# A shared PSUM copy and a closed-up product order in a Winograd-style matrix product

## The chip, the cores and the metric

The kernel runs on one core of one Trainium2 chip. The metric is the device time of one execution in microseconds, the median of several runs. One execution is also recorded by the hardware profiler; its instruction times are what the profile shows.

## The reference

Input `x` is 8 × 3584 tokens of 192 channels. A causal depthwise convolution with 7 taps (8 heads, softmax of the taps) comes first. Each token is then sent to one of 8 experts, and the expert is a two-layer network with 1024 hidden units. Cut to what matters:

```python
# convolution: out[s] = sum over k of softmax(weight)[head, k] * x[s + k - 6]
logits = x @ w_gate                          # (B, S, 8)
local_gate = sigmoid(x @ w_local)
for b in range(B):
    for s in range(S):
        fresh_e = argmax(logits[b, s])
        e = fresh_e if s == 0 or local_gate[b, s] < 0.5 else prev_e
        prev_e = e
        p = softmax(logits[b, s])
        h = maximum(x[b, s] @ w1[e], 0.0)     # 192 -> 1024
        out[b, s] = p[e] * (h @ w2[e])        # 1024 -> 192
```

## The kernel before, in words

All is float32. The 28672 tokens are taken in 16 groups of 1792. For each group the kernel convolves on VectorE (`conv`, line 423, with one small step per head on ScalarE, line 413), computes the gate and the place of every token on VectorE (`route`), and scatters the tokens' rows by GpSimd into a table in device memory sorted by expert (`put`, line 828). TensorE multiplies blocks of 128, 256 or 512 tokens of one expert. Blocks 0 to 27 have 128 tokens, 28 to 70 have 256, **71 to 93 have 512** (the large blocks), and smaller ones follow. Convolution and routing of later groups ("side work") run on VectorE beside the products of blocks that are already complete.

The order on each engine is the order in which the code issues its instructions (a manual schedule); nothing is moved by a planner. How much side work stands at a place of a block is set by budgets: `step(t)` takes steps of routing or convolution until their nominal costs reach `t` us, and an overdraft is taken off the next call. In a large block there are four such calls, with the budgets `SIDE = (2.4, 4.5, 2.0, 1.8)`: the first inside the hidden layer's product (not in block 71), the second behind it, the third and fourth in the output product, behind each half's first eviction. Side work is done when the last group's tables are made.

A large block goes as follows.

- `turn_late` (line 1135) transposes the block's rows on VectorE; `combine_x` (lines 1186 to 1191) makes the sums of token pieces there, `combine_w` (lines 1168 to 1172, 1177) the sums of weight pieces on GpSimd.
- `seven` (lines 1194 to 1247) makes the hidden layer. Of the three 64-channel pieces of the input two are multiplied by seven products in place of eight, in Winograd's way, and the third is added. `times` (line 1208, matmuls at line 1211) issues eight matmuls: two column pieces `j`, two row halves; each row half has a PSUM bank of its own. Three PSUM tiles of two banks are used: `xb`, `yb` (both named `ps` in the profile) and `wbk` (named `xps`). `xb` holds running sums: ScalarE copies it after the first product (line 1217) into `h11` and after the second (line 1225) into `h12`; then the third product is accumulated on it. `h22` is copied from `yb` (line 1223).
- Between the second product and the third, `wbk` takes eight matmuls of `a12, b21` and four of `a13, b31`; the other four of these follow the third product. Then VectorE adds (`h22` at line 1231, `h11` at 1233, `h12` at 1243) and ScalarE applies the ReLU (lines 1235, 1244 to 1246). The weight and token pieces `t2`, `s2` and so on, the hidden pieces, all lie in tiles that the profile names `xg`, `hot`, `hT`.
- `output_late` (matmuls at line 1261) makes the output layer in two halves of 256 tokens; ScalarE (line 1271) and VectorE (line 1276) scale the results, and GpSimd scatters them to the output (line 1096). `ensure` loads the rows of the blocks ahead on SP (lines 986, 991), once their tokens are scattered.

Of the kernel before, what the change touches and what calls it, by code (L numbers as in the profile page):

```python
# [111 lines left out]
def kernel(  # L112
# [10 lines left out]
    nc = tc.nc  # L123
# [264 lines left out]
    def halves():  # L388
        return [(half, slice(half * DR, (half + 1) * DR)) for half in range(2)]
# [431 lines left out]
    def put(behind=None):  # L821


        if not to_put:
            return
        g, rows, to = to_put.pop(0)
        nc.gpsimd.nop()
        ins = nc.gpsimd.indirect_dma_start(  # L828
            out=slots[:, :], in_=rows, in_offset=None,
            out_offset=bass.IndirectOffsetOnAxis(ap=to, axis=0)).ins  # L830
        if behind is not None:
            tc.add_manual_dep(ins, behind.ins.name, SYNC, reason="scatters apart")
        if puts:
            tc.declare_no_dep(ins, group="puts", reason="slots of their own")
        if g:
            tc.declare_no_dep(ins, group="gets", reason="those slots were full before")
        puts.append((g, ins))
        tc.add_to_no_dep_group("puts", ins)
        tc.add_to_no_dep_group(f"puts{g}", ins)
# [299 lines left out]
    def pieces(n):  # L1139


        return [room[f"h{k}"][:, :4 * n * P].rearrange("p (h j s) -> p h j s", h=2, j=2)
                for k in range(4)]
# [50 lines left out]
    def seven(wb, wt, weight_then, xT, xc, rows_then, weights_next):  # L1194


        one, two = slice(0, HU * P), slice(HU * P, KQ * P)
        h11, h12, h21, h22 = pieces(HU)
        b11, t1, b21, b22, b31, b32 = [wb[:, WB + k * 2 * P:WB + (k + 1) * 2 * P]
                                       for k in range(6)]  # L1200
        t2, t3, t4 = wt
        a11, s1, a12, a22, a13, a23 = [xT[:, d, s] for d in range(KD) for s in (one, two)]
        s3, s2, s4, s5 = xc
        xb, wbk, yb = [pool.tile([P, 2, 512], F32, name=name).rearrange(
            "p h (j s) -> p h j s", j=2)
            for pool, name in ((late_p[0], "ps"), (xps_p, "xps"), (late_p[1], "ps"))]

        def times(to, a, b, first=False, js=range(2)):
            for j in js:
                for half, rows in halves():  # L1210
                    ins = nc.tensor.matmul(to[:, half, j, :], lhsT=b[rows, j * P:(j + 1) * P],  # L1211
                                           rhs=a[rows, :], start=(first and j == 0), stop=True,
                                           skip_group_check=True)
            return ins

        weight_then(times(xb, a11, b11, True))
        nc.scalar.copy(h11, xb)
        ins = times(yb, s1, t1, True)
        if held:
            held.pop(0)(ins)  # L1220
        rows_then()
        times(yb, a23, b32)
        nc.scalar.copy(h22, yb)
        times(xb, s2, t2)
        nc.scalar.copy(h12, xb)
        put(times(wbk, a12, b21, True))
        times(wbk, a13, b31, js=[0])
        if st["block"] > FIRST:
            step(SIDE[0], early=1)
        put(times(xb, s3, t3))  # L1230
        nc.vector.tensor_tensor(h22, xb, h22, op=Alu.add)
        times(wbk, a13, b31, js=[1])
        nc.vector.tensor_tensor(h11, wbk, h11, op=Alu.add)  # L1233
        for side in range(2):
            nc.scalar.activation(h11[:, side], h11[:, side], Act.Relu)  # L1235
        times(yb, s4, b22)
        put(times(yb, s5, b32))
        times(xb, a22, t4)
        wt = weights_next()
        next(wt)  # L1240
        put(times(xb, a23, b31))
        next(wt)
        nc.vector.tensor_tensor(h12, yb, h12, op=Alu.add)
        nc.scalar.activation(h12, h12, Act.Relu)
        nc.scalar.activation(h21, xb, Act.Relu)
        nc.scalar.activation(h22, h22, Act.Relu)
        return [[h11, h12], [h21, h22]], wt

    def output_late(n, wb, xg, hT, rows_next=None, between=None):

        for part, h in enumerate(hT):
# [21 lines left out]
            if n == KQ:  # L1273
                step(SIDE[2 + part], late_p[0] if part == 0 else None)
            for k in range(m):
# [10 lines left out]
    late_p = []  # L1286
    LEAD = 2
    LATE = 3
    SIDE = (2.4, 4.5, 2.0, 1.8)
    st = {"block": 0, "conv": 1, "cgen": None, "route": 1, "rgen": None, "routed": 1,  # L1290
          "due": False, "hot": False, "since": 0, "bank": None, "over": 0}

    def start_conv():
        g = st["conv"] + 1

        free = not any(p[0] <= g - 3 for p in to_put)
        if (st["cgen"] is None and g < NPART and g <= st["route"] + LEAD and free
                and (g != 3 or g in x_in and st["block"] > LATE + 2)):
            st["conv"] = g
            st["cgen"] = conv(g, x_in.pop(g))  # L1300
            next(st["cgen"])

    def conv_op():
        c = next(st["cgen"], None) if st["cgen"] else None
        if c is None:
            st["cgen"] = None
        return c

    def start_route():
        done = st["conv"] - (st["cgen"] is not None)  # L1310
        if st["rgen"] is None and st["route"] < done:
            st["route"] += 1
            st["rgen"] = route(st["route"])

    def route_op():
        c = next(st["rgen"], None)
        if c is None:
            st["rgen"] = None
            st["routed"] = PADS if st["route"] == LAST else st["route"]
        return c  # L1320

    def step(time, bank=None, early=0, force=False):

        start_route()
        start_conv()
        go = st["rgen"] is not None
        if st["due"]:
            go = (not late_p and st["block"] < FIRST - 1
                  or bank is not None and (force or st["since"] < st["block"]))
            if go:  # L1330
                st["due"], st["bank"] = False, bank
        time += st["over"]
        while time > 0:
            c = route_op() if go else conv_op()
            if c is None:
                if not go:
                    break
                go = False
            elif c == "pe":
                st["due"], st["since"], go = True, st["block"] - early, False  # L1340
            elif c == "hop":
                go = False
            elif c == "placed":
                pass
            else:
                time -= c + 0.05 if go and late_p else c
        st["over"] = min(time, 1.5) if late_p else 0
# [87 lines left out]
    for i, (_, n, _, _) in enumerate(blocks):  # L1435
# [12 lines left out]
        def weights_next():  # L1448
            return combine_w(wbs[i + 1]) if n_next == KQ else iter([None] * 5)
# [25 lines left out]
        if n == KQ:  # L1475
            hT, wt = seven(wbs[i], wt, weight_then, xT, xc, lambda: ensure(i), weights_next)
        else:
            hT = hidden_late(n, wbs[i], xT)
        if n_next:
            xT = turn_late(n_next, xgs[i + 1][0])  # L1480
        if n == KQ:
            step(SIDE[1])
        wts, xcs = [], []
# [116 lines left out]
```

## Time and profile before

| | |
|---|---|
| median of 3 runs | 1312.17 us (1308.29 to 1316.62) |
| profiled execution, its own time | 1309.78 us |
| its span, first to last instruction | 1308.1 us |
| granted TensorE clock | 0.998 |
| large blocks | 695.8 to about 1177 us |
| TensorE matmuls at line 1211 in `seven` | 2024, 88 in each of 23 blocks |
| copy of the second sum, line 1225 | 23 times, 1.02 us each |

The profile gives one execution. A row of the timeline holds the start in us, the length in us, the engine, the line, the operation, the tile written and those read, and how many instructions are merged into it; in brackets the idle time of the engine ahead of it and what ended it. PE is TensorE's matmuls, PEld its weight loads, DVE VectorE, ACT ScalarE, POOL GpSimd, SP the queue that issues loads. A row of groups holds the count, the busy time, the mean length in ns, and the idle time ahead of the group with what ended most of it. A row of waits names who waited for whom, the total in us, the number of times, and sometimes the longest. A row on one line gives the shortest, median and longest instruction in ns.

### The profile page before, as it was taken

To read this page: it belongs to the slowest core of one execution; us is meant where nothing else is said; L and a number is where in the kernel's file an instruction comes from. 1 tells how busy PE (TensorE), PEld (TensorE's weight loads), DVE (VectorE), ACT (ScalarE), POOL (GpSimd) and SP (SyncE) were. 2 spreads that over 40 slices of the span, in tenths; PEclk is the share of its full clock that TensorE was granted. 3 is DMA by queue.
4 is the path that set the end of the run, shared out by engine and by line. 5 is a ranking of instruction groups with operands and counts; after the bars stand their busy time and mean duration, and the time that the engine had idled before them with its cause. 6 is when DMAs were issued, how large, how long until landed. Compare 5 with 4: busy or idle time off the path is not lost. (4 is left out here: it accounts for less than half of the span.)

```text
span 1308.1 us, 39979 instructions
## 1 busy us (share of the span) xinstructions
PE 1276.2 (98%) x15750; PEld 1206.7 (92%) x15750; DVE 956.1 (73%) x2602; ACT 617.5 (47%) x1407; POOL 553.1 (42%) x619
## 2 busy tenths in 40 slices
PE   9899999999999999999999999999999999999997
PEld 7798999999999999899999899999999899999996
DVE  5888898889888788788988998898857844431111
ACT  5345555445555645456463454454434434342332
POOL 4444443534344444444435633654462664421211
PEclk9999999999999999999999999999999999999999
DMA  5789988857767767667696655555455637536894
GB/s 197 272 342 387 373 345 347 296 201 270 259 213 263 257 219 259 215 231 259 206 282 174 181 163 154 149 150 151 125 171 113 194 108 189 155 95 193 268 326 156
DMA packets 130243, 291.18 MB, mean 223 GB/s; under 512 B 87936, under 2 KB 104759, under 8 KB 114306
## 3 DMA queue, kind: packets, MB, share of 16 engines
q1 hardware_dynamic: 107728, 243.35, 56.6%
q0 software_dynamic: 22320, 45.22, 10.2%
q8 instruction: 126, 2.06, 0.7%
q14 instruction: 67, 0.55, 0.1%
q10 hardware_dynamic: 2, 0.00, 0.0%
HBM read 242.92 MB, written 46.07 MB: 221 GB/s over the span
## 5 line engine op out<-in xcount | busy, mean ns | idle before, releaser
L423 DVE SCALAR_TENSOR_TENSOR y_sb<-x_sb,c,y_sb 128x336 f32<-128x336 f32 x672 | 384.5, 581 | 33.3 <-ACT y_sb L413 11.0
L1068 PE MATMUL yps<-wb,hT 64*128 64x192 f32 x3648 | 318.6, 326 | 5.2 <-ACT hT L1056 3.0
L1047 PE MATMUL hps<-xT,wb 64*128 64x256 f32 (+1 forms) x3408 | 315.4, 336 | 2.6 <-issue 1.3
L828 POOL DMA_INDIRECT slots<-y_sb,posi x228 | 227.9, 1000 | 208.9 <-PE yps L1068 150.3
L1261 PE MATMUL ps<-wb,hot 64*128 64x192 f32 x3680 | 309.7, 324 | 2.1 <-issue 1.8
L1261 PEld LDWEIGHTS ps<-wb,hot 64*128 64x128 f32 x3680 | 299.3, 187 | 9.4 <-ACT hot L1235 5.0
L1068 PEld LDWEIGHTS yps<-wb,hT 64*128 64x128 f32 x3648 | 297.4, 187 | 10.2 <-ACT hT L1056 5.1
L1047 PEld LDWEIGHTS hps<-xT,wb 64*128 64x128 f32 x3408 | 283.2, 187 | 23.6 <-issue 3.6
L1096 POOL DMA_INDIRECT out_dram<-o_sb,head x115 | 120.6, 1049 | 296.7 <-DVE o_sb L1276 270.9
L1056 ACT ACTIVATE hT<-hps 128x512 f32<-128x512 f32 (+1 forms) x284 | 130.4, 510 | 161.0 <-PE hps L1047 116.5
L1096 POOL DMA_INDIRECT out_dram<-o_sb,xg x114 | 117.1, 1028 | 207.8 <-DVE o_sb L1082 112.4
L1271 ACT ACTIVATE o_sb<-ps,head 128x192 f32<-128x192 f32 x115 | 43.0, 418 | 205.2 <-PE ps L1261 178.9
L1276 DVE SCALAR_TENSOR_TENSOR o_sb<-ps,head,o_sb 128x192 f32<-128x192 f32 x115 | 43.2, 411 | 111.2 <-ACT o_sb L1271 108.6
L1029 ACT COPY xT<-xps 64x256 f32<-64x256 f32 (+4 forms) x284 | 105.1, 370 | 9.5 <-PE yps L1068 2.2
L1078 ACT ACTIVATE o_sb<-yps,xg 128x192 f32<-128x192 f32 x114 | 43.3, 418 | 125.2 <-PE yps L1068 96.9
L1135 DVE STREAM_TRANSPOSE xT<-y_sb 128x768 f32<-128x768 f32 (+1 forms) x65 | 54.8, 870 | 61.7 <-PE ps L1156 31.2
L1211 PE MATMUL ps<-xT,wb 64*128 64x256 f32 x736 | 88.5, 377 | 1.0 <-DVE xT L1187 1.0
L1211 PEld LDWEIGHTS ps<-xT,wb 64*128 64x128 f32 x736 | 75.3, 187 | 4.9 <-issue 2.2
L1082 DVE SCALAR_TENSOR_TENSOR o_sb<-yps,xg,o_sb 128x192 f32<-128x192 f32 x114 | 43.4, 412 | 33.1 <-ACT o_sb L1078 27.5
L1235 ACT ACTIVATE hot<-hot 128x512 f32<-128x512 f32 x46 | 26.4, 622 | 83.6 <-DVE hot L1233 61.1
L1156 PE MATMUL ps<-xT,wb 64*128 64x128 f32 (+1 forms) x912 | 64.5, 294 | 0.5 <-DVE xT L1135 0.5
L1156 PEld LDWEIGHTS ps<-xT,wb 64*128 64x128 f32 x912 | 62.6, 188 | 1.2 <-DVE xT L1135 1.1
(281 smaller groups left out, 1337.8 us busy)
## 6 DMA issues: line engine op xcount, KB each, us to landing
wb<-in_w_dram SPq DMA_DIRECT2D x109, 1536.0 KB
x_sb<-in_x_dram SPq DMA_DIRECT2D x14, 1920.0 KB
y_sb<-slots SPq DMA_DIRECT2D x92, 192.0 KB
xg<-slots SPq DMA_DIRECT2D x43, 195.0 KB
wb<-in_w_dram SPq DMA_DIRECT2D x12, 512.0 KB
slots<-y_sb,posi POOLq DMA_INDIRECT x228
x_sb<-in_xb_dram SPq DMA_DIRECT2D x4, 768.0 KB
y_sb<-slots SPq DMA_DIRECT2D x60, 48.0 KB
```

The source lines that it names most:

```text
L423: nc.vector.scalar_tensor_tensor(cols(h), chans(h, k), c[:, h, k:k + 1], cols(h), Alu.mult, Alu.add)
L828: ins = nc.gpsimd.indirect_dma_start(out=slots[:, :], in_=rows, in_offset=None, out_offset=bass.IndirectOffsetOnAxis(ap=to, axis=0)).ins
L1029: copied = nc.scalar.copy(a, b)
L1047: ins = nc.tensor.matmul(hps[half][:, j, w], lhsT=wb[rows, f0:f0 + P], rhs=xT[rows, d, w], start=(d == 0 and j == 0), stop=(d == KD - 1), ...
L1056: nc.scalar.activation(hT[:, m:m + 2, w], hps[half][:, :, w], Act.Relu)
L1068: ins = nc.tensor.matmul(yps[half][:, k * D:(k + 1) * D], lhsT=hT[rows, m, k * P:(k + 1) * P], rhs=wb[rows, WA + m * D:WA + (m + 1) * D], ...
L1082: nc.vector.scalar_tensor_tensor(o_sb[:, k, :], y[k][1], xg[:, k, 0:1], o_sb[:, k, :], Alu.mult, Alu.add)
L1096: sent = nc.gpsimd.indirect_dma_start(out=out, in_=o, in_offset=None, out_offset=bass.IndirectOffsetOnAxis(ap=xg.bitcast(I32)[:, k, 1:2], ...
L1135: nc.vector.transpose(xT.rearrange("p d (j t) -> p j d t", t=Q)[:, js], rows[:, js].rearrange("p j (d t) -> p j d t", t=Q))
L1156: nc.tensor.matmul(hps[:, half, j, :], lhsT=wb[rows, f0:f0 + P], rhs=xT[rows, d, :], start=(d == 0 and j == 0), stop=(d == KD - 1), skip_g ...
L1211: ins = nc.tensor.matmul(to[:, half, j, :], lhsT=b[rows, j * P:(j + 1) * P], rhs=a[rows, :], start=(first and j == 0), stop=True, skip_gro ...
L1261: ins = nc.tensor.matmul(yps[:, half, k * D:(k + 1) * D], lhsT=h[two][rows, side, j, k * P:(k + 1) * P], rhs=wb[rows, f * D:(f + 1) * D], ...
```

## The change

In `seven`, the copy of the second sum is cut in two: ScalarE copies the first bank of `xb` into the first half of `h12`, VectorE the second bank into the second half. VectorE's half is issued behind the first stretch of side work of the block. That stretch is issued earlier in the code, ahead of the products into `wbk`, and its budget goes from 2.4 to 1.8. The third product is issued behind the eight matmuls of `a12, b21`; all eight matmuls of `a13, b31` follow it.

```diff
-        def times(to, a, b, first=False, js=range(2)):
-            for j in js:
+        def times(to, a, b, first=False):
+            for j in range(2):
                 for half, rows in halves():
...
         times(xb, s2, t2)
-        nc.scalar.copy(h12, xb)
-        put(times(wbk, a12, b21, True))
-        times(wbk, a13, b31, js=[0])
+        nc.scalar.copy(h12[:, 0], xb[:, 0])
         if st["block"] > FIRST:
             step(SIDE[0], early=1)
+        nc.vector.tensor_copy(h12[:, 1], xb[:, 1])
+        put(times(wbk, a12, b21, True))
         put(times(xb, s3, t3))
         nc.vector.tensor_tensor(h22, xb, h22, op=Alu.add)
-        times(wbk, a13, b31, js=[1])
+        times(wbk, a13, b31)
         nc.vector.tensor_tensor(h11, wbk, h11, op=Alu.add)
...
-    SIDE = (2.4, 4.5, 2.0, 1.8)
+    SIDE = (1.8, 4.5, 2.0, 1.8)
```

## The prediction

> **What bounds the kernel now.** I read the page first: who is busy, and where in the span.
>
> ```profile
> PE 1276.2 (98%) x15750; PEld 1206.7 (92%) x15750; DVE 956.1 (73%) x2602; ACT 617.5 (47%) x1407; POOL 553.1 (42%) x619
> ...
> PE   9899999999999999999999999999999999999997
> ...
> DVE  5888898889888788788988998898857844431111
> ```
>
> TensorE is the bound from end to end, so an edit is worth what it adds to or takes from TensorE's waits. VectorE is busy eight tenths until slice 33, so whatever is given to it there stands in a queue. The change sits in the 23 large blocks (I number them 71 to 93, as in the list of blocks), which fill 695.8 to 1177. Next I read the timeline of one that has no side work, block 88:
>
> ```profile
> 1059.45 1.49 PE L1211 MATMUL xps<-xT,wb 64*128 64x256 f32 x12
> ...
> 1059.78 1.02 ACT L1225 COPY hot<-ps 128x1024 f32<-128x1024 f32 x1
> ...
> 1060.85 1.13 PE L1211 MATMUL ps<-xg 64*128 64x256 f32 x8
> ...
> 1061.82 0.60 PE L1211 MATMUL xps<-xT,wb 64*128 64x256 f32 x4
> ...
> 1062.10 1.23 DVE L1231 TENSOR_TENSOR hot<-ps,hot 128x1024 f32<-128x1024 f32 x1 [4.37 <-PE ps L1211]
> ...
> 1062.25 1.89 PE L1211 MATMUL ps<-hT,wb 64*128 64x256 f32 x16
> ...
> 1063.98 1.03 PE L1211 MATMUL ps<-xT,xg 64*128 64x256 f32 x8
> ...
> 1064.84 1.03 PE L1211 MATMUL ps<-xT,wb 64*128 64x256 f32 x8
> ...
> 1065.71 0.49 PEld L1261 LDWEIGHTS ps<-wb,hot 64*128 64x128 f32 x6 [0.24 <-ACT hot L1235]
> 1065.74 0.60 PE L1261 MATMUL ps<-wb,hot 64*128 64x192 f32 x4
> ```
>
> Call A the start of the twelve filler matmuls (1059.45). Sixteen matmuls take 1.73 us (1062.25 to 1063.98), so one costs 0.108 and twelve 1.30. The third product starts at A+1.40 as soon as the 1.02 us copy L1225 lets go of the second sum. So the copy costs 0.10 us in this block; the filler hides the rest. L1231 follows at A+2.65, the output product at A+6.29.
>
> ```profile
> PEld ps L1211 <- ACT hot L1225: 8.2, 23, 1.5
> ```
>
> The chain of waits makes it look bigger: 8.2 us in 23 waits, 0.36 each. That is weight-load idle; of block 88's share 0.10 is lost pace. 23 blocks at 0.10 are **2.3 us, about all there is to win** in undisturbed blocks.
>
> **The copy, halved.** Durations for 128x512 out of PSUM:
>
> ```profile
> L1056 ACT ACTIVATE hT<-hps 128x512 f32<-128x512 f32 x172 | 93.0, 594 | 111.0 <-PE hps L1047 94.9 <-remote 9.0 <-PE xps L394 7.1
> ```
> ```profile
> L269 ACT COPY z<-hps x9: 532/533/550, 12.5 to 27.5; 128x448 f32<-128x448 f32 x9
> L269 DVE COPY z<-hps x3: 624/625/625, 12.1 to 15.3; 128x448 f32<-128x448 f32 x3
> ```
>
> ScalarE's half: 0.59. VectorE's half is not in the trace: at least the 0.625 of 448 columns, at most 0.71 in proportion; I take 0.69. ScalarE's half would be done at 1059.78+0.59, and with the 0.05 us from copy end to matmul today (1060.80 to 1060.85) the third product starts at A+0.97 at best, since the shorter filler (eight matmuls, 0.86) is out earlier. Then come 8 matmuls (0.97, with the gap that follows a wait), 8+16+8+8 (4.31): output at A+6.25, against A+6.29. **Gain per undisturbed block: 0.04 us.** The smaller filler takes back nearly all that the faster copy gives. The four matmuls moved behind the third product cost nothing: L1233 needs them only after L1231, 1.2 us later. The step of side work itself now stands ahead of the first filler's scatter and of its matmuls. It issues VectorE's steps, ScalarE's small ones (L413, L642), which follow the copy on ScalarE's queue as before, and now and then a load on SP; it puts nothing on GpSimd's queue, and nothing on TensorE's, because this call gives it no PSUM bank. So its move passes no queue in which another order results; only VectorE's queue changes, by the copy.
>
> **The wait that is added.** VectorE's half stands in VectorE's queue behind the first stretch of side work (convolution and routing of later tokens, nominal 2.4 us now, 1.8 after). Behind that copy stands L1231, which needs the third product; so TensorE now waits for side work that it could ignore before. How late VectorE is, is told by its idle time ahead of L1231:
>
> ```profile
> L1231 DVE TENSOR_TENSOR hot<-ps,hot x23: 1211/1225/1225, 701.8 to 1163.2; 128x1024 f32<-128x1024 f32 x23
> ...
> PE ps L1211: 48.6, 21
> ```
> ```profile
> 701.84 1.23 DVE L1231 TENSOR_TENSOR hot<-ps,hot 128x1024 f32<-128x1024 f32 x1 [1.30 <-PE ps L1211]
> ```
> ```profile
> 788.61 1.23 DVE L1231 TENSOR_TENSOR hot<-ps,hot 128x1024 f32<-128x1024 f32 x1 [2.11 <-PE ps L1211]
> ```
> ```profile
> 956.36 1.23 DVE L1231 TENSOR_TENSOR hot<-ps,hot 128x1024 f32<-128x1024 f32 x1 [3.71 <-PE ps L1211]
> ```
> ```profile
> 978.58 1.22 DVE L1231 TENSOR_TENSOR hot<-ps,hot 128x1024 f32<-128x1024 f32 x1 [2.20 <-PE ps L1211]
> ```
> ```profile
> 1163.19 1.23 DVE L1231 TENSOR_TENSOR hot<-ps,hot 128x1024 f32<-128x1024 f32 x1 [4.37 <-PE ps L1211]
> ```
>
> With an idle time g, VectorE is free at A+2.65−g today. After: 0.6 earlier, plus 0.69 for the copy and 0.05, so the third product starts at A+2.79−g. It breaks even at A+1.01 (A+6.29 less 5.28). **So g has to be 1.78 us; each microsecond short of it is lost on TensorE.** Of the 48.6 us, 6×4.37 belong to blocks 88 to 93, 3.71 to block 83 and 1.30 to block 71 (none with side work ahead of L1231); 17.4 remain for 13 blocks, 1.34 on average. Two blocks, 72 and 73, have no idle time at all.
>
> The sum on TensorE:
> - 13 blocks: 13 × (1.78−1.34) = +5.7. Blocks 75 and 84 (2.11, 2.20) cannot bank their surplus: +0.7. In some blocks the output product already waits today for the chain that L1231 opens, and the change gives that chain room (0.97+0.86 us of products behind the third, against 0.97+0.43):
>
> ```profile
> PEld ps L1261 <- ACT hot L1235: 5.0, 16, 0.6
> ```
>
>  5.0 less 16 × 0.24 (block 88's, part of the pace): −1.2.
> - Block 72:
>
> ```profile
> 720.54 3.37 DVE L423 SCALAR_TENSOR_TENSOR y_sb<-x_sb,c,y_sb 128x336 f32<-128x336 f32 x4
> ...
> 721.82 1.14 PE L1211 MATMUL ps<-xg 64*128 64x256 f32 x8 [0.36 <-ACT hot L1225]
> ...
> 723.83 1.22 DVE L1231 TENSOR_TENSOR hot<-ps,hot 128x1024 f32<-128x1024 f32 x1
> ```
> ```profile
> 727.45 1.86 PE L1261 MATMUL ps<-wb,hot 64*128 64x192 f32 x19 [0.27 <-issue]
> ```
>
>  Four convolution steps fill VectorE until 723.83. One step fewer (0.57) and the copy (0.69) put the third product at about 724.0, the output at 729.3: +1.8. Block 73 looks the same (L1231 at 745.60 without idle time), but a later TensorE lets VectorE catch up: between 0.6 and 1.8, taken as +1.2.
> - Block 71 has no side work to shorten:
>
> ```profile
> 700.12 0.42 DVE L1191 TENSOR_TENSOR hT<-xT 128x256 f32<-128x256 f32 x1
> ```
> ```profile
> 705.48 0.76 PE L1261 MATMUL ps<-wb,hot 64*128 64x192 f32 x6
> ```
>
>  Free at 700.54, copied at 701.23, output at 706.56: +1.1.
> - Seven blocks without side work: 7 × −0.04 = −0.3.
> - The shorter stretch. 0.6 us less in each of some 16 blocks is 9.6 us of side work moved back, against a budget of 10.1 a block: it ends about a block later. Counting the side work's steps off against the budgets (each step carries its nominal cost in the code), block 83's first stretch, empty today, gets three transposes of 0.95:
>
> ```profile
> L606 DVE STREAM_TRANSPOSE z<-y_sb 128x768 f32<-128x768 f32 x42 | 38.3, 953 | 0.4
> ```
>
>  Between 0 and 1.2 for that; taken as +0.6. The last group's scatters slip too; block 90 is the first to need them:
>
> ```profile
> 1087.72 1.84 DVE L1135 STREAM_TRANSPOSE xT<-y_sb 128x768 f32<-128x768 f32 x2 [1.91 <-DMA y_sb<-slots]
> ```
> ```profile
> 1092.89 0.41 DVE L1186 TENSOR_TENSOR xg<-xT 128x256 f32<-128x256 f32 x1
> ```
>
>  The transposes end 3.3 us ahead of the first use: one more scatter, and the load behind it, fit there. Nothing.
>
> Together 5.7+0.7−1.2+1.8+1.2+1.1−0.3+0.6 = **+9.6 us**. The profiled execution took 1309.78 (span 1308.1): 1319.4, said as **1319**. The median shown is 1312.17, 2.4 above it, within the 1308.29 to 1316.62 of its runs; by it the same sum gives 1321.8.
>
> Two prices stay open. Does GpSimd slow the copy? The side work's steps stretch beside it:
>
> ```profile
> L423 DVE SCALAR_TENSOR_TENSOR y_sb<-x_sb,c,y_sb x112: 528/571/1541, 713.9 to 942.4; 128x336 f32<-128x336 f32 x112
> ```
>
> 0.57 grows to 1.54 in the worst case, but L1231, which reads PSUM, keeps 1.211 to 1.225 in all 23. I take no stretch; one of 0.97 in each of some 13 blocks would be +12.6 on top, 1332, the upper end. [...] The lower end: were the copy always in time, 23 × −0.04, −1.2 and 72 and 73 at up to −1.0 each (the pace gap at their output) come to −4.
>
> **Rivals.** (1) **VectorE is in time.** If side work's real steps land early, TensorE never waits for VectorE's half and all blocks look like 88: −4 to +2, about 1308. For it: g averages 2.1 over all 23, ScalarE loses 0.42 us a block, and the changed stretch holds other steps than today's. Against: only 9 of 23 blocks have g of 1.78 or more. [...]
>
> ```profile
> 715.95:737.90 21.95, 20.97 (x219) 19.18 (x218) 20.38 (x32) 9.48 (x14) 13.21 (x14) 1.00 0.54 154
> ...
> 908.30:928.50 20.20, 20.20 (x220) 19.20 (x218) 17.97 (x60) 8.45 (x12) 7.95 (x9) 1.00 0.51 139
> ...
> 1056.00:1076.20 20.20, 20.20 (x219) 19.20 (x218) 8.76 (x14) 8.45 (x12) 12.71 (x14) 1.00 0.37 128
> ```
>
> (stretch, its length, then busy time of PE, PEld, DVE, ACT, POOL.) [...] (2) **VectorE becomes the bound.** Between its copy and L1231 it must now idle about 1.3 us (third product and hand-over, 1062.10−1060.85), and side work cannot use that. Where busy time plus 1.3 plus today's other waits exceeds the block, lateness is carried over, as between 72 and 73. From a block of 20.2 it decides at about 18.5 busy, close to the 17.97 above. All 15 side-work blocks behind 72 at block 73's 1.2 make 18, with 72 (1.8) and 71 (1.1): +21, about 1331. (3) The change doesn't do what it says, because the wait for ScalarE's half remains: that is in the 0.97 above, and gives no time of its own.
>
> **The numbers.** Forecast (+3 to +13): 0.58. Rival 1: 0.24. Rival 2: 0.18. Range 1306 (rival 1) to 1332 (rival 2, and the stretched copy). One per cent, 13 us, is about what a measurement of this kernel tells from no change. None of the cases reaches 13 us faster: 0.02. Slower by more: rival 2 and the forecast's upper edge counted from the median, 0.27. Within: 0.71.
>
> **What the profile after would show.** If right: L1231's idle time near 1.2 us in every side-work block, TensorE's wait ahead of the third product put down to VectorE's copy, 0.69 us long, of some 0.5 us in most of blocks 71 to 82 and gone from 89 on, where a block is 20.18 long. ScalarE's half 0.59. Side work in block 88. Wrong if the copy starts right after the second sum in most blocks (rival 1), or if VectorE runs without idle time from block to block (rival 2); or if block 90 waits for its rows.

## The result and the profile after

The changed kernel took 1329.63 us (median of 4 runs, 1329.38 to 1331.55) against 1312.58 for the kernel before on the same chip: ratio **1.0134, 95% interval 1.0100 to 1.0167**. The profiled execution took 1331.55 us, with a span of 1329.6.

The page of the kernel after, busy time and the slices:

```profile
PE 1278.4 (96%) x15750; PEld 1205.2 (91%) x15750; DVE 972.9 (73%) x2625; ACT 607.5 (46%) x1407; POOL 551.4 (41%) x619
...
PE   9899999999999999999998999899999999999996
...
DVE  5888898888888888788887988898857774431111
```

TensorE has about the same work, 1278 us against 1276, in a longer span, so most of the time was lost in waits. Where it was lost is told by the first product of block 71 and of block 93 in the timelines. Before:

```profile
695.81 1.47 PE L1211 MATMUL ps<-xT,wb 64*128 64x256 f32 x12
...
1157.08 2.14 PE L1211 MATMUL ps<-xT,wb 64*128 64x256 f32 x18
```

After:

```profile
694.53 2.75 PE L1211 MATMUL ps<-xT,wb 64*128 64x256 f32 x24
...
1175.11 1.25 PE L1211 MATMUL ps<-xT,wb 64*128 64x256 f32 x10
```

From the one to the other it is 461.27 us before and 480.58 after: **+19.3 of the +21.5 us of span lie in the large blocks** of these two executions (the medians differ by 17). The rest is 1.3 less ahead of the large blocks and 3.5 more behind, of which 2.2 is one wait for a load in a small block. The kernel before doesn't have this wait, nor does a second profile of the kernel after (e9 below):

```profile
PE ps L1156 <- DMA y_sb<-slots: 2.2, 1, 2.2
```

An undisturbed block, one without side work around the copy, shows the new state. Block 93 in the timeline after, with A again the start of the filler:

```profile
1178.56 1.03 PE L1211 MATMUL xps<-xT,wb 64*128 64x256 f32 x8
...
1178.88 0.59 ACT L1225 COPY hot<-ps 128x512 f32<-128x512 f32 x1
...
1179.50 0.69 DVE L1228 COPY hot<-ps 128x512 f32<-128x512 f32 x1 [2.67 <-ACT hot L1225]
...
1180.25 1.13 PE L1211 MATMUL ps<-xg 64*128 64x256 f32 x8 [0.65 <-DVE hot L1228]
1181.21 1.03 PE L1211 MATMUL xps<-xT,wb 64*128 64x256 f32 x8
1181.43 1.23 DVE L1231 TENSOR_TENSOR hot<-ps,hot 128x1024 f32<-128x1024 f32 x1 [1.24 <-PE ps L1211]
```

Read the brackets. VectorE is idle for 2.67 us and has nothing else to do, yet its half of the copy starts 0.03 us after *ScalarE's half ends* (1178.88+0.59=1179.47), not when the second sum is ready. **The halves run one after the other.** Two short copies in a row (0.59+0.69) take longer than the one of 1.02 that they replace, and the filler ahead of the third product is shorter by four matmuls. So the third product starts at A+1.69 (1180.25−1178.56) in place of A+1.40, and TensorE waits 0.65 us. The undisturbed block, 20.22 us long before and 20.18 in the forecast, is 20.82 long.

The waits after, and the three VectorE and ScalarE groups on this path:

```profile
PEld ps L1211 <- DVE hot L1228: 30.9, 23, 2.9
...
DVE hot L1231 <- PE ps L1211: 27.5, 21, 2.2
...
DVE hot L1228 <- ACT hot L1225: 21.7, 12, 2.7
PE ps L1211 <- DVE hot L1228: 21.7, 23, 2.5
```
```profile
L1225 ACT COPY hot<-ps x23: 585/592/592, 698.2 to 1178.9; 128x512 f32<-128x512 f32 x23
L1228 DVE COPY hot<-ps x23: 647/691/692, 699.2 to 1179.5; 128x512 f32<-128x512 f32 x23
...
L1231 DVE TENSOR_TENSOR hot<-ps,hot x23: 1224/1225/1225, 701.1 to 1181.4; 128x1024 f32<-128x1024 f32 x23
```

TensorE now waits in all 23 blocks, 21.7 us in sum. In 12 of them VectorE stood idle until ScalarE's half ended; in the other 11 its queue came free only as ScalarE's half ended or later, as forecast. (The 21.7 us in the row of VectorE's wait is its own idle time, and most of that it would have had anyhow; that the two totals are equal is chance.) Both mechanisms are in this one profile, and the runs below take them apart.

Why do the halves not overlap? Each reads another bank of one PSUM tile. The program holds the second of them by a semaphore until the first has ended, although both only read that tile; e3 and e12 below show that it is this order and not the memory. A row of the profile *before* shows it already, at a place where VectorE (line 297) and ScalarE (line 298) copy the two halves of one PSUM tile:

```profile
ACT wb L298 <- DVE wb L297: 1.7, 1, 1.7
```

ScalarE waited there 1.7 us for a copy by VectorE whose result it doesn't use. I had not read this row.

In both places the two copies also write parts of one tile (`hot`, `wb`), so the order could come from that side. Two other rows of the profile before speak against it. Line 269 copies one PSUM tile after another into parts of one tile `z`, and there the two engines overlap (VectorE until 14.82, ScalarE from 14.59):

```profile
14.20 0.62 DVE L269 COPY z<-hps 128x448 f32<-128x448 f32 x1 [0.35 <-PE hps L267]
14.59 0.53 ACT L269 COPY z<-hps 128x448 f32<-128x448 f32 x1 [0.23 <-PE hps L267]
```

So it is the common PSUM tile that fits. No run here gives the two halves PSUM tiles of their own, which would be the direct test.

### The profile page after: what moved, and what is told of

The parts are those of the page before. It is cut to its first block, busy times and chain, and to the rows that moved or that the text cites. A ratio compares the mean times of both kernels' runs of the same rounds, so it can differ in the third digit from the quotient of the medians.

```text
span 1329.6 us, 40013 instructions
## 1 busy us (share of the span) xinstructions
PE 1278.4 (96%) x15750; PEld 1205.2 (91%) x15750; DVE 972.9 (73%) x2625; ACT 607.5 (46%) x1407; POOL 551.4 (41%) x619
## 5 line engine op out<-in xcount | busy, mean ns | idle before, releaser
L423 DVE SCALAR_TENSOR_TENSOR y_sb<-x_sb,c,y_sb 128x336 f32<-128x336 f32 x672 | 384.8, 582 | 33.4 <-ACT y_sb L413 10.8
L1211 PEld LDWEIGHTS ps<-xT,wb 64*128 64x128 f32 x736 | 71.1, 187 | 6.7
L1211 PE MATMUL ps<-xg 64*128 64x256 f32 x368 | 52.0, 402 | 25.6 <-DVE hot L1228 21.7
L1211 PEld LDWEIGHTS ps<-xg 64*128 64x128 f32 x368 | 34.5, 190 | 39.6 <-DVE hot L1228 30.9
```

The lines of the kernel that those rows point to most:

```text
L423: nc.vector.scalar_tensor_tensor(cols(h), chans(h, k), c[:, h, k:k + 1], cols(h), Alu.mult, Alu.add)
```

## The experiments

Theory 1: the serial copies cost the time. Theory 2: VectorE's half is late behind the side work (the forecast). All ratios are to the kernel before on the same chip, with 95% intervals; times in us that are worked out from ratios are taken of a kernel before of 1306.55 us, the median on the chip of e1 to e4. The edits are against the kernel after where nothing else is said.

**e1_apart**: the order between the two halves is taken away (they read different banks and write different halves).

```diff
-        nc.scalar.copy(h12[:, 0], xb[:, 0])
+        left = nc.scalar.copy(h12[:, 0], xb[:, 0])
...
-        nc.vector.tensor_copy(h12[:, 1], xb[:, 1])
+        right = nc.vector.tensor_copy(h12[:, 1], xb[:, 1])
+        tc.declare_no_dep(right.ins, left.ins, reason="another bank")
```

> The changed kernel, but VectorE's half of the copy no longer has to wait for ScalarE's half (they read different PSUM banks). Theory 1 (serial halves: VectorE's half is held until ScalarE's has ended): the 12 waits of 21.7 us on VectorE vanish; the third product comes 0.7 us earlier in blocks 84, 85, 87 and 89 to 93, 0.4 to 0.6 in 80 and 82, together about 7.5 us: 1322, and an undisturbed block is 20.2 long instead of 20.8. Theory 2 (side work ahead of VectorE's half in its queue makes up the loss): nothing changes, 1329 to 1330, since the half is late anyway.

Measured 1.0112 (1.0092 to 1.0133): less of a gain than theory 1 expected (1322 is a ratio of 1.007), and within the interval of the kernel after. Its waits:

```profile
PE ps L1211 <- DVE hot L1228: 13.7, 12, 2.6
PE ps L1211 <- ACT hot L1225: 1.7, 2, 0.9
```

The wait for VectorE fell from 23 blocks to 12. With 0.7 us in block 79, which the profile puts down to another instruction of ScalarE, TensorE's wait ahead of the third product is 16.2 us. Undisturbed blocks are 20.24 long, as theory 1 expected, but in those with side work VectorE is late, up to this in block 78:

```profile
849.55 0.59 ACT L1225 COPY hot<-ps 128x512 f32<-128x512 f32 x1
849.92 1.93 DVE L423 SCALAR_TENSOR_TENSOR y_sb<-x_sb,c,y_sb 128x336 f32<-128x336 f32 x2
...
851.77 0.68 DVE L1228 COPY hot<-ps 128x512 f32<-128x512 f32 x1
...
852.60 1.13 PE L1211 MATMUL ps<-xg 64*128 64x256 f32 x8 [2.58 <-DVE hot L1228]
```

VectorE's copy has no bracket: its engine was busy until then, here with two convolution steps that took 1.93 us in place of the usual 2×0.57. This is the forecast's mechanism by itself.

**e2_early**: the order stays, but VectorE's half is issued ahead of the side work.

```diff
         nc.scalar.copy(h12[:, 0], xb[:, 0])
+        nc.vector.tensor_copy(h12[:, 1], xb[:, 1])
         if st["block"] > FIRST:
             step(SIDE[0], early=1)
-        nc.vector.tensor_copy(h12[:, 1], xb[:, 1])
```

> The changed kernel with VectorE's half issued ahead of the first stretch of side work instead of behind it; the wait for ScalarE's half is kept. Theory 2 (queue): TensorE no longer waits for side work, all blocks near 20.2, about 1313. Theory 1 (serial halves): the third product still can't start before A+1.65, undisturbed blocks stay 20.8 long; only the blocks in which VectorE was free later than ScalarE's end (71, 73 to 79, 81) gain, 0.1 to 1.1 each, about 4 us: 1325 or 1326.

Measured 1.0133 (1.0112 to 1.0154), about the whole loss, and above both expectations (1325 or 1326 for theory 1 is a ratio of 1.010). Its waits:

```profile
DVE hot L1226 <- ACT hot L1225: 48.0, 21, 3.5
...
PE ps L1211 <- DVE hot L1226: 17.4, 23, 1.8
```

VectorE now stands idle at the head of its own queue until ScalarE's half ends, 48 us in sum, and TensorE still waits in all 23 blocks. (Most of the 48 us is no loss: in an undisturbed block 2.02 of 2.67 us pass before the second sum is ready, as e3 shows.) Undisturbed blocks are 20.82 long, as theory 1 expected. The queue is gone, and nothing is won that can be measured.

**e3_apart_early**: both edits.

```diff
-        nc.scalar.copy(h12[:, 0], xb[:, 0])
+        left = nc.scalar.copy(h12[:, 0], xb[:, 0])
+        right = nc.vector.tensor_copy(h12[:, 1], xb[:, 1])
+        tc.declare_no_dep(right.ins, left.ins, reason="another bank")
         if st["block"] > FIRST:
             step(SIDE[0], early=1)
-        nc.vector.tensor_copy(h12[:, 1], xb[:, 1])
```

> Both edits at once: halves independent, VectorE's half ahead of the side work. If the two theories together are all of the loss: third product at A+0.97, undisturbed blocks 20.2 long, about the time of the kernel before (1311 to 1314). If the shorter filler or the shorter budget of the first stretch carries part of the loss, 1316 or more.

Measured **1.0029 (1.0017 to 1.0040)**: most of the loss is gone, but not all; e5 shows what the shorter filler costs by itself. The undisturbed block in the timeline, then the waits:

```profile
1160.98 1.06 PE L1211 MATMUL xps<-xT,wb 64*128 64x256 f32 x8
...
1161.28 0.69 DVE L1226 COPY hot<-ps 128x512 f32<-128x512 f32 x1 [2.02 <-PE ps L1211]
1161.31 0.59 ACT L1225 COPY hot<-ps 128x512 f32<-128x512 f32 x1
...
1162.12 1.13 PE L1211 MATMUL ps<-xg 64*128 64x256 f32 x8
```
```profile
PEld ps L1211 <- ACT hot L1225: 12.3, 22, 1.7
...
PE ps L1211 <- DVE hot L1226: 2.3, 2, 1.4
...
PE ps L1211 <- ACT hot L1225: 1.1, 1, 1.1
```

The copies run side by side in their full pace, and TensorE's wait ahead of the third product is 3.4 us. Set against it: late queue alone (e1) 16.2 us, serial halves alone (e2) 17.4, both (after) 21.7. Above e3's 3.4 that is 12.8, 14.0 and 18.3, where the sum of the first two would be 26.8: **the third product waits for the later of the two, so each hides part of the other.** That is why removing either alone moved the time so little: 1.0134 to 1.0112 or 1.0133. Removing the second one, once the first is gone, is worth 0.83% (e1 to e3, 10.8 us; the medians say 9.3) or 1.04% (e2 to e3, 13.6 us; the medians say 11.8).

**e4_budget**: the kernel before with `SIDE[0]` 1.8 in place of 2.4, and nothing else. The diff is against the kernel before.

```diff
-    SIDE = (2.4, 4.5, 2.0, 1.8)
+    SIDE = (1.8, 4.5, 2.0, 1.8)
```

> The kernel before with nothing changed but the budget of the first stretch of side work, 1.8 in place of 2.4. As predicted (side work ends a block later, at no more than 1.2 us): 1312 to 1314. Rival (the later scatters hold up the rows of block 90, and logits fall into worse places): 1316 or more. Neither theory 1 nor 2 plays here.

Measured 1.0006 (0.9995 to 1.0017): 0.8 us, which can't be told from nothing.

**e5_order**: the whole copy on ScalarE, so that only the product order and the budget differ from before.

```diff
-        nc.scalar.copy(h12[:, 0], xb[:, 0])
+        nc.scalar.copy(h12, xb)
...
-        nc.vector.tensor_copy(h12[:, 1], xb[:, 1])
```

> The changed kernel with the copy whole again on ScalarE: what is left of the change is the shorter filler (eight matmuls ahead of the third product, eight of the other group behind it) and the budget of 1.8. If the filler is the price: third product at A+1.40 as in the kernel before, but four more matmuls behind it, so an undisturbed block is 20.6 long instead of 20.2, 23 x 0.4 = 9 us, ratio 1.007. If the filler costs nothing (those four matmuls fill other gaps): ratio 1.000 to 1.002.

Measured 1.0042 (1.0026 to 1.0059), between the two expectations. An undisturbed block:

```profile
1146.69 1.03 PE L1211 MATMUL xps<-xT,wb 64*128 64x256 f32 x8
1147.01 1.02 ACT L1225 COPY hot<-ps 128x1024 f32<-128x1024 f32 x1
1148.08 1.14 PE L1211 MATMUL ps<-xg 64*128 64x256 f32 x8 [0.35 <-ACT hot L1225]
```

The third product starts at A+1.39, as before, but eight matmuls (0.86) now cover the copy where twelve (1.30) did. The four that were moved behind it lengthen the rest: 20.52 us a block in place of 20.22. Where they stood before, they filled time in which TensorE would have waited for the copy.

**e6_both_scalar**: both halves on ScalarE, one behind the other.

```diff
         nc.scalar.copy(h12[:, 0], xb[:, 0])
+        nc.scalar.copy(h12[:, 1], xb[:, 1])
...
-        nc.vector.tensor_copy(h12[:, 1], xb[:, 1])
```

> The changed kernel with both halves of the copy on ScalarE, one behind the other; VectorE has no part. Serial halves: 0.33 + 1.15 us, third product at A+1.54, block 20.75, ratio about 1.009 to 1.010, close to the changed kernel, whose halves are serial too. If VectorE's queue is what costs: clearly nearer to the kernel before than that, 1.002 or less.

Measured 1.0056 (1.0040 to 1.0072), somewhat less than expected: the second half starts 0.47 us behind the first, before its 0.59 are over (the starts in one block are 1148.18 and 1148.65), so cutting a copy in two on one engine costs about 0.07 a block (20.59 against 20.52). The serial pair on two engines doesn't overlap in this way (0.03 us from one half's end to the other's start, 20.82 a block), and is dearer.

**e7_best** and **e8_best18**: the product order of before (twelve matmuls ahead of the third product), independent halves, VectorE's ahead of the side work; the budget is 2.4 in e7 and 1.8 in e8.

```diff
         times(xb, s2, t2)
-        nc.scalar.copy(h12, xb)
+        left = nc.scalar.copy(h12[:, 0], xb[:, 0])
+        right = nc.vector.tensor_copy(h12[:, 1], xb[:, 1])
+        tc.declare_no_dep(right.ins, left.ins, reason="another bank")
         put(times(wbk, a12, b21, True))
         times(wbk, a13, b31, js=[0])
```

(The diff is against the kernel before.)

> The kernel before (twelve matmuls ahead of the third product, budget 2.4) with the copy cut in two independent halves, VectorE's issued ahead of the side work. The copy ends at A+1.0, below the filler's A+1.30, so the third product never waits: undisturbed blocks 20.1 long, gain 0.1 in some 15 blocks; against it VectorE is 0.69 later in its side work in front of L1231. Expected ratio 0.998 to 1.002: nothing to win, because the copy was all but hidden.

> The same with the budget of the first stretch at 1.8, which gives VectorE back 0.6 us in front of L1231. If VectorE's lateness is what the 0.69 us cost in e7: 0.996 to 0.999; if the budget doesn't matter for the time: as e7.

Measured 1.0029 (1.0018 to 1.0039) for e7, a little outside what I expected, and **0.9983 (0.9968 to 0.9998)** for e8. In both the undisturbed block is 20.02 us, 0.20 less than before; e8's shows why:

```profile
1139.40 1.49 PE L1211 MATMUL xps<-xT,wb 64*128 64x256 f32 x12
1139.71 0.69 DVE L1226 COPY hot<-ps 128x512 f32<-128x512 f32 x1 [2.01 <-PE ps L1211]
1139.74 0.59 ACT L1225 COPY hot<-ps 128x512 f32<-128x512 f32 x1
...
1140.70 1.06 PE L1211 MATMUL ps<-xg 64*128 64x256 f32 x8
```

TensorE doesn't wait here: the third product comes at A+1.30, right behind the twelve. But VectorE has 0.69 us more to do ahead of L1231. Block 72 in e7:

```profile
710.64 0.69 DVE L1226 COPY hot<-ps 128x512 f32<-128x512 f32 x1 [0.39 <-PE ps L1211]
711.25 2.89 DVE L423 SCALAR_TENSOR_TENSOR y_sb<-x_sb,c,y_sb 128x336 f32<-128x336 f32 x4
...
714.06 1.22 DVE L1233 TENSOR_TENSOR hot<-ps,hot 128x1024 f32<-128x1024 f32 x1
...
715.42 1.13 PE L1211 MATMUL ps<-xT,xg 64*128 64x256 f32 x8 [0.57 <-DVE hot L1233]
```

L1233 in this kernel is the addition that was L1231. It starts 1.26 us later than TensorE would let it (A+3.72, with the filler's start at 710.34, against A+2.46 in an undisturbed block), and the products into the same PSUM tile wait for it. Here the budget of 1.8 pays, which by itself (e4) was worth nothing.

**e9_after_again**, the kernel after without a change, on another chip:

> The changed kernel as it is, beside the other kernels of this set on one chip. Both theories: the ratio of its first measurement, 1.0134, again (1.012 to 1.015), with undisturbed blocks 20.8 long.

Measured 1.0156 (1.0133 to 1.0179), in agreement with 1.0134, and undisturbed blocks are 20.82 long.

**e10_fix71** (e8, but block 71 keeps the whole copy on ScalarE, since VectorE's half starts there only at A+1.19) and **e11_fix71_12** (e10 with another budget). The diffs are against e8 and e10:

```diff
+        if st["block"] == FIRST:
+            nc.scalar.copy(h12, xb)
+        else:
             left = nc.scalar.copy(h12[:, 0], xb[:, 0])
...
-    SIDE = (1.8, 4.5, 2.0, 1.8)
+    SIDE = (1.2, 5.1, 2.0, 1.8)
```

> As e8 (independent halves, VectorE's ahead of the side work, twelve matmuls of filler, budget 1.8), but block 71, where VectorE is free only 1.3 us after the filler's start, keeps the whole copy on ScalarE. Expected: block 71 20.1 long instead of 20.8, the rest as e8: ratio 0.997 to 0.998. If e8's gain was chance: 1.000.

> As e10 with the first two budgets at 1.2 and 5.1 (same sum as 1.8 and 4.5). If VectorE's lateness ahead of L1231 is what still lengthens blocks 72, 83 and 86 (0.4 to 1.0 us each in e8): 0.996 to 0.997. If the work only comes to stand in another place, before the copy of the next block: as e10.

Measured 0.9990 (0.9978 to 1.0001) and 0.9987 (0.9976 to 0.9998). Block 71 is 20.14 long in both, as expected, but neither time is better than e8's. The gain expected of e10 didn't come, and its interval takes in 1.000, the case that e8's gain was chance; e11 is as e10, its second case, with an interval just below 1. No version here beats the kernel before by more than about 0.2%.

**e12_swap**: e2 with the halves issued in the other order, VectorE's first (a single run).

```diff
+        nc.vector.tensor_copy(h12[:, 1], xb[:, 1])
         nc.scalar.copy(h12[:, 0], xb[:, 0])
...
-        nc.vector.tensor_copy(h12[:, 1], xb[:, 1])
```

> As e2, but VectorE's half is issued first and ScalarE's second, with nothing else changed. Theory 1, in the form that whichever half is issued second waits for the other because both read one PSUM tile: now VectorE's half starts at A+0.3 and ScalarE's only at its end, A+1.0, third product at A+1.64. If instead VectorE alone was held (its own queue or its slower start): both run from A+0.3, third product at A+1.1.

One run of 1304.38 us against a median of 1291.56, some 1.0%. The timeline:

```profile
1155.06 0.69 DVE L1225 COPY hot<-ps 128x512 f32<-128x512 f32 x1 [2.01 <-PE ps L1211]
1155.78 0.59 ACT L1226 COPY hot<-ps 128x512 f32<-128x512 f32 x1 [0.59 <-DVE hot L1225]
1156.42 1.13 PE L1211 MATMUL ps<-xg 64*128 64x256 f32 x8 [0.62 <-ACT hot L1226]
```

The wait has turned round: now ScalarE waits for VectorE, and the third product starts at A+1.65 (the filler starts at 1154.77), where theory 1 had A+1.64. So it hangs on the order of issue and not on either engine, which is what an order between readers of one tile predicts. That the two engines can't read these banks at once is ruled out by e3, whose copies of them overlap for 0.59 us without getting longer (0.69 and 0.59).

## Why the prediction was right and where it failed

The forecast of 1319 had the sign, and its range held the time. It was 10.6 us short of the median after. In differences: +9.6 us were forecast, and the medians differ by 17.05, above the forecast's own band of +3 to +13. The range reached so far because of rival 2 and the stretched copy, and neither came: VectorE stood idle ahead of its half in 12 of the 23 blocks, and its copy kept to 0.69 us. That the range held is in part luck. The late queue was right; what was missing beside it is this.

- **The step that failed: "the third product starts at A+0.97 at best", and from it "Gain per undisturbed block: 0.04 us".** It took the halves to run side by side. They ran in a row, the third product came at A+1.69, and an undisturbed block lost 0.60 us. Of the term "Seven blocks without side work: 7 × −0.04 = −0.3" six (88 to 93) were in truth 0.60 longer or more, 3.6 in place of −0.2; the seventh, block 83, had got side work. The same floor stood under the other blocks: none has its third product earlier than A+1.60. With the queue out of the way (e2 to e3) this step alone is worth 13.6 us.
- **It is not all that was missing.** e1 is the kernel that the forecast had in mind, with halves that don't wait for each other, and it is 14.6 us (12.0 to 17.4) slower than before, not 9.6. Of the 5 us between, 2.6 are the late queue (below); the other 2.4 are in e3, which stays 3.8 us slower where the rest of the sum (+1.1, −0.3, +0.6) has 1.4. Each of these two parts is within the noise by itself, and what makes them up isn't shown. From e1 to the kernel after it is 2.9 us by the first measurement and 5.7 by e9, with intervals that overlap or touch: most of the serial wait is hidden behind the late queue.
- **A lower clock had no term.** Behind two waits of 2.25 and 2.50 us in the profile after TensorE ran slower (granted clock 0.60 and 0.53 in the first 2 us), which made 3.4 us; behind e1's wait of 2.58 the clock stayed at 1.00. The last section has the rows.
- **Rival 3 named the right wait and threw it away.** "the wait for ScalarE's half remains: that is in the 0.97 above, and gives no time of its own" holds only if VectorE's half doesn't wait for it as well.
- **The late queue was right.** Its terms (+5.7, +0.7, −1.2, +1.8, +1.2) make 8.2; measured alone (e1 to e3) it is 10.8. In the kernel after it is partly hidden under the serial wait. "gone from 89 on, where a block is 20.18 long" failed with the first step: e1 has 20.24 there, the kernel after 20.82.
- **L1231's idle time** was to be near 1.2 in every side-work block: it was 1.24 in all but blocks 72 and 78, where it was 1.87 and 2.17 and TensorE itself ran at a lower clock (below).
- **Durations.** ScalarE's half 0.59 and VectorE's 0.69, both right, with no stretch beside GpSimd (0.692 at most): the upper end's +12.6 never came. That the matmul follows the copy's end by 0.05 us failed in a small way. In e3 the copies end at 1161.97 and 1161.90, and the third product starts at 1162.12, 0.15 behind the later one; why it takes longer there isn't shown. So even independent halves gave A+1.14, not 0.97, and an undisturbed block of 20.25, not 20.18.
- **The shorter stretch**, taken as +0.6: e4 measures 0.8 us (−0.7 to +2.2), which says neither 0.6 nor 0. Side work did move back a block; block 88 has some now.
- **Block 90's rows**, priced at nothing: right, but with less room than thought. Timeline after:

```profile
1107.00 1.84 DVE L1135 STREAM_TRANSPOSE xT<-y_sb 128x768 f32<-128x768 f32 x2 [4.99 <-DMA y_sb<-slots]
```

VectorE's wait for them grew from 1.91 to 4.99 us, and TensorE began the block without waiting.
- **About all there is to win** was put at 2.3 us (0.10 a block). e8's undisturbed blocks win 0.20: the third product starts 0.10 earlier, and takes 1.06 in place of 1.13, with no wait of TensorE ahead of it. So the bound was half of what such a block gave. e8's time wins 0.17%, 2.2 us; that this equals the 2.3 is luck, as other blocks lost what these won more. Most of the copy was hidden already.

## What to carry to other kernels

Before a copy is shared between two engines, look in the profile for a place where two engines already read one PSUM tile, and see whether the one waits for the other: here separate banks did not help while the program ordered the reads (1.0133 in e2, 1.0029 in e3 without the order). When two new waits stand ahead of the same instruction, that instruction waits for the later one, so an experiment that removes one of them says little (1.0112 and 1.0133 here, against 1.0029 without both); remove both, then add each back. And work that is handed to a busy engine must be placed in its queue: the same 0.69 us copy, issued behind the side work and not ahead of it, made the kernel 0.83% longer (e1 against e3).

## What the runs showed of the hardware that I had not expected

In e3 ScalarE and VectorE read two banks of one PSUM tile at once, and their copies took 0.59 and 0.69 us, as they did one after the other in the kernel after.

Behind two waits, of 2.25 and 2.50 us, TensorE came back at a lower clock in the profile after. Its stretches (length, busy time of PE, PEld, DVE, ACT and POOL, granted clock, DMA), in block 78:

```profile
854.00:857.00 3.00, 0.57 (x6) 0.17 (x2) 2.96 (x5) 1.30 (x3) 2.79 (x3) 1.00 0.97 372
857.00:859.00 2.00, 1.93 (x10) 1.61 (x12) 0.01 (x1) 0.00 (x0) 1.25 (x2) 0.53 1.19 239
859.00:861.50 2.50, 2.50 (x20) 2.13 (x18) 1.93 (x2) 0.00 (x0) 0.96 (x1) 0.69 1.17 220
861.50:876.00 14.50, 14.50 (x248) 13.78 (x246) 13.11 (x23) 5.70 (x10) 7.50 (x8) 1.00 0.10 34
```

Behind its wait of 2.50 us the granted clock was 0.53, then 0.69, and the eight matmuls of the third product took 2.07 us in place of 1.13. In block 72, behind 2.25 us, it was 0.60, then 0.69:

```profile
723.60:725.50 1.90, 1.86 (x10) 1.58 (x12) 0.04 (x1) 0.00 (x0) 0.29 (x1) 0.60 1.11 299
725.50:728.60 3.10, 3.10 (x22) 2.58 (x22) 2.40 (x2) 0.18 (x1) 0.95 (x1) 0.69 1.05 219
```

From the third product to the output it was 6.97 us in blocks 72 and 78, and 5.28 in most others: 3.4 us of the loss in this profile. Behind two other long waits, 2.13 here (block 83) and e1's 2.58, shown above, the clock stayed at 1.00, as it did in this profile behind the 20 waits of 0.54 to 1.67 us. So it is not the length of the wait alone; what else decides it no run here shows. e1's third product took the usual 1.13, in this stretch:

```profile
852.00:855.00 3.00, 2.40 (x22) 2.43 (x24) 1.61 (x3) 0.00 (x0) 2.39 (x3) 1.00 1.16 265
```
